# A fused attention and token-mixing kernel: q in 6 KB rows, x transposes inside attention, later loads on ScalarE's queue

## The chip, the cores and the metric

One core of one Trainium2 chip. The metric is the device time of one execution in microseconds (us), as the median of several. A run counts as slow when it is over 1.5% above the fastest of the same kernel. The rounds ran on different chips, so each run is compared with before in its own rounds. A difference of under 2% is called "within 2%".

## The reference, cut to what matters

Attention with 16 query heads and 4 key heads over 8 batches of 384 tokens (head size 64), whose result x (384 x 1024 per batch) goes through a token mixer: two thin projections, a 384 x 384 token matrix made of them, a rectifier, and a 1024 x 1024 output projection.

```python
scores = scale * np.matmul(q, k.transpose(0, 1, 3, 2))     # per head
attn = softmax(scores); attn_out = np.matmul(attn, v)
x = attn_out.transpose(0, 2, 1, 3).reshape(B, S, H * D)    # 8 x 384 x 1024
wq = x @ w_q; wk = x @ w_k                                 # 1024 -> 64
W_tok = scale * np.einsum('bsd,btd->bst', wq, wk)
mixed = np.einsum('bst,btd->bsd', W_tok, x)
return np.maximum(mixed, 0.0) @ w_out
```

## The kernel before

The program is a list scheduler in Python: it keeps estimated clocks of the engines and decides in which fixed order TensorE gets its work. Per batch, 36 scores matmuls fill 18 slots of PSUM (the memory, in banks, that TensorE writes its results to) that ScalarE turns into exponentials, 12 groups of 12 matmuls by v follow, and VectorE divides each group by its row sums and writes it to `xnat` in SBUF (the on-chip memory of the operands) as bf16. The tokens are spread so that partition p holds the tokens 3p, 3p+1 and 3p+2. The parts that the argument needs:

```python
def load(b):                       # all on SyncE's queue; q rows of 3 x 64 floats, 768 bytes
    def ld(dst, src, a, z, c0=0, c1=C):
        nc.sync.dma_start(out=dst[:, a:z, c0:c1],
                          in_=src[b, a:z].rearrange("h (p c) d -> p h c d", p=P)[:, :, c0:c1])
...
def attend(b, g, u):               # 12 times a batch
    xnats[b] = x_p.tile([P, C, Hq, D], BF16, name="xnat", bufs=3)
    ...
    avv = ps[:, :G * DE].rearrange("p (i e) -> p i e", i=G)
    nc.vector.reciprocal(out=rcp, in_=avv[:, :, D])
    nc.vector.tensor_tensor(out=xnats[b][:, c, h0:h0 + G, :], in0=avv[:, :, :D],
                            in1=rcp.to_broadcast([P, G, D]), op=ALU.mult)   # 256 neighbours
...
def po():                          # output projection and store
    dst = out[b].rearrange("(p c) n -> c p n", c=C)[c]      # 128 rows of 4 KB
    ...
    nc.sync.dma_start(out=dst, in_=osb)
...
wld[:, dc:dc + 2, :] <- moe_w_out[dc * P:(dc + 2) * P, :].rearrange("(c p) n -> p c n", p=P)   # shortened
```

The softmax here doesn't subtract the row's maximum and nothing guards it: scores larger than these inputs give would overflow.

## Time and profile before

| | before |
|---|---|
| median of 3 runs | 224.09 us (223.12 to 225.83) |
| span of the profiled execution | 224.3 us |
| TensorE / VectorE / ScalarE busy | 95% / 65% / 63% |

(The profiled execution took 226.12 us in all and counts as a slow one, so its waits may be a little longer than those of a median run; there is no other profile of before.) The prediction below shows the page's head and the hole at 42.6 to 45.4 us. First, from the page's costliest groups (line, engine, operation, tiles, count, then busy us, mean ns of one, and idle time before it), the two steps of VectorE that finish a group of heads:

```profile
L289 DVE TENSOR_TENSOR xnat<-bank,rcp 128x256 bf16<-128x256 f32 x96 | 40.8, 425 | 3.3
L287 DVE RECIPROCAL rcp<-bank 128x4 f32<-128x4 f32 x96 | 16.9, 176 | 17.6 <-PE bank L282 16.7
```

Second, the busy time of each engine in two whole batches of the steady part (from the first scores of one batch to those of the next):

```profile
core 0: us, PE busy (x) PEld busy (x) DVE busy (x) ACT busy (x) POOL busy (x), PEclk, DMA share, GB/s
91.30:113.00 21.70, 21.38 (x248) 11.32 (x252) 15.49 (x41) 17.39 (x19) 5.32 (x10) 1.00 1.04 258
113.00:134.70 21.70, 21.38 (x245) 11.26 (x248) 14.15 (x39) 17.44 (x19) 5.32 (x10) 1.00 1.08 233
```

A steady batch takes 21.7 us and TensorE is busy in 21.4 of them; over four such batches (68.7 to 156.3 us, 21.9 us each) VectorE works 15.5 us a batch, 71%. That is more than its 65% of the span, since the whole includes stretches where it has little to do.

### The profile page before, as it was taken

How to read it: one execution, taken by the hardware profiler on the slowest of the kernel's cores; microseconds unless marked ns; L12 is line 12 of the kernel's file. 1: busy time of each engine (PE TensorE's matmuls, PEld its weight loads, DVE VectorE, ACT ScalarE, POOL GpSimd, SP SyncE). 2: the span in 40 equal slices, each digit the busy share in tenths (PEclk: the TensorE clock that was granted, in tenths of full speed). 3: DMA queues.
4: the chain of work that ended last, by engine and by line, in shares of the span. 5: the costliest groups of instructions: out<-in, count | busy, mean ns of one | idle time of the engine just before them, and what ended most of it. 6: DMA issues, size and time to landing. Idle time of an engine off the chain costs nothing.

```text
span 224.3 us, 5470 instructions
## 1 busy us (share of the span) xinstructions
PE 214.2 (95%) x2217; PEld 113.6 (51%) x2244; DVE 145.2 (65%) x365; ACT 140.6 (63%) x146; POOL 52.1 (23%) x97
## 2 busy tenths in 40 slices
PE   8999999589999999999999999999999999999993
PEld 5666665245545545454555546554555553434441
DVE  2355786834697758865887648874679569576332
ACT  3599998747788778887887887887888600000000
POOL 1385678406300540045016100620000000000000
PEclk9999999959999999999999999999999999999999
DMA  6996999999399979999999998989224422242424
GB/s 174 324 327 170 410 386 325 136 237 323 65 183 215 335 166 187 222 338 216 223 229 342 154 213 260 281 205 154 99 91 53 143 93 93 93 190 93 180 101 187
DMA packets 71688, 46.09 MB, mean 205 GB/s; under 512 B 42736, under 2 KB 67568, under 8 KB 71664
## 3 DMA queue, kind: packets, MB, share of 16 engines
q1 hardware_dynamic: 71520, 45.62, 77.6%
q8 instruction: 17, 0.28, 0.5%
q10 hardware_dynamic: 144, 0.13, 0.2%
q14 instruction: 7, 0.06, 0.1%
HBM read 23.59 MB, written 12.58 MB: 161 GB/s over the span
## 4 chain that ended last, share of the span: by engine, by line
PE 74%; DMA 14%; DVE 3%; SPq 3%; POOL 3%; issue 1%; DVEq 0%
PE bank L408 37%; PE bank L282 13%; PE sc L259 12%; DMA qraw<-in_q_dram 12%; PE bank L331 4%; SPq L129 3%; PE bank L384 3%; PE bank L362 2%; DMA QT<-qb 2%; PE bank L322 1%; POOL qb L158 1%; DVE osb L421 1%; PE bank L349 1%; DVE msb L389 1%; POOL wqk_sb L596 1%
## 5 line engine op out<-in xcount | busy, mean ns | idle before, releaser
L263 ACT ACTIVATE pt<-sc 128x1024 bf16<-128x1024 f32 x144 | 138.9, 1023 | 34.6 <-PE sc L259 34.4
L408 PE MATMUL bank<-wout_sb,msb 128*128 128x512 bf16 x357 | 91.7, 382 | 1.3 <-issue 0.5
L408 PEld LDWEIGHTS <-msb 128*128 128x128 bf16 x384 | 33.8, 98 | 42.4 <-issue 13.7
L259 PE MATMUL sc<-QT,KT 64*128 64x512 bf16 x288 | 47.5, 387 | 3.1 <-DMA QT<-qb 2.9
L282 PEld LDWEIGHTS <-pt 128*128 128x128 bf16 x1152 | 41.9, 98 | 15.8 <-issue 9.9
L282 PE MATMUL bank<-vext,pt 128*128 128x65 bf16 x1152 | 46.9, 195 | 0.4 <-DVE osb L421 0.2
L421 DVE COPY osb<-bank 128x512 f32<-128x512 f32 (+1 forms) x49 | 33.1, 677 | 21.7 <-PE bank L408 20.5
L289 DVE TENSOR_TENSOR xnat<-bank,rcp 128x256 bf16<-128x256 f32 x96 | 40.8, 425 | 3.3
L389 DVE TENSOR_SCALAR msb<-bank 128x384 bf16<-128x384 f32 x64 | 32.5, 551 | 9.5 <-PE bank L384 9.0
L287 DVE RECIPROCAL rcp<-bank 128x4 f32<-128x4 f32 x96 | 16.9, 176 | 17.6 <-PE bank L282 16.7
L158 POOL CAST qb<-qraw 128x768 bf16<-128x768 f32 x30 | 24.0, 827 | 17.4 <-DMA qraw<-in_q_dram 15.1
L153 POOL CAST kb<-kraw 128x192 bf16<-128x192 f32 x30 | 9.2, 347 | 67.3 <-DMA kraw<-in_k_dram 67.3
L259 PEld LDWEIGHTS <-KT 64*128 64x128 bf16 x288 | 12.4, 94 | 24.1 <-issue 17.2
L117 PE MATMUL bank<-idle 128*128 128x256 bf16 x80 | 14.8, 324 | 1.0 <-DVE idle L562 1.0
L331 PE MATMUL bank<-xT,wqk_sb 128*128 128x384 bf16 x64 | 11.7, 327 | 0.0
L117 PEld LDWEIGHTS <-idle 128*128 128x128 bf16 x80 | 7.9, 114 | 6.6 <-issue 4.0
L384 PE MATMUL bank<-wT,Csb 64*128 64x384 bf16 x32 | 10.6, 332 | 0.4 <-DVE rcp L287 0.3
L384 PE MATMUL bank<-wq,Csb 64*128 64x384 bf16 x32 | 10.6, 332 | 0.0
L599 POOL CAST wout_sb<-wld 128x1024 bf16<-128x1024 f32 x8 | 8.1, 1040 | 4.1 <-DMA wld<-in_moe_w_out_dram 4.1
L366 DVE CAST Csb<-bank 128x512 bf16<-128x512 f32 x8 | 5.5, 688 | 5.2 <-PE bank L362 5.2
L337 DVE CAST wT<-bank 128x384 bf16<-128x384 f32 x8 | 4.5, 558 | 6.7 <-PE bank L331 6.7
L323 DVE COPY xT<-bank 128x1024 bf16<-128x1024 bf16 x10 | 6.9, 688 | 2.5 <-PE bank L322 2.5
(33 smaller groups left out, 70.1 us busy)
## 6 DMA issues: line engine op xcount, KB each, us to landing
out_dram<-osb SPq DMA_DIRECT2D x23, 512.0 KB, 3.1
qraw<-in_q_dram SPq DMA_DIRECT2D x15, 768.0 KB, 7.4
wld<-in_moe_w_out_dram SPq DMA_DIRECT2D x4, 1024.0 KB, 9.5
kraw<-in_k_dram SPq DMA_DIRECT2D x7, 384.0 KB, 4.3
vraw<-in_v_dram SPq DMA_DIRECT2D x7, 384.0 KB, 8.9
qraw<-in_q_dram SPq DMA_DIRECT2D x1, 512.0 KB, 5.3
kraw<-in_k_dram SPq DMA_DIRECT2D x2, 192.0 KB, 3.7
vraw<-in_v_dram SPq DMA_DIRECT2D x2, 192.0 KB, 6.3
```

The costliest lines, as they stand in the source:

```text
L117: nc.tensor.matmul(out=bank_ps[i][:, :256], lhsT=idle[:, :P], rhs=idle, start=True, stop=True)
L158: eng.tensor_copy(out=nats[b][1][:, :, kp, :, u, :].rearrange("p c i d -> p i c d"), in_=raws[b][2][:, h0:h0 + G])
L259: nc.tensor.matmul(out=ps[:, u, :], lhsT=KT[lo:hi, kp * C + kc, :], rhs=QT[lo:hi, t0:t0 + G, :].rearrange("k i p -> k (i p)"), start=True, ...
L263: nc.scalar.activation(out=pt.rearrange("k u i p -> k u (i p)"), in_=ps, func=AF.Exp, scale=attn_scale)
L282: nc.tensor.matmul(out=ps[:, i * DE:i * DE + D + 1], lhsT=tiles[kc][:, u, i, :], rhs=vext[:, 2 * kp + u, kc, :D + 1], start=(kc == 0), sto ...
L287: nc.vector.reciprocal(out=rcp, in_=avv[:, :, D])
L289: nc.vector.tensor_tensor(out=xnats[b][:, c, h0:h0 + G, :], in0=avv[:, :, :D], in1=rcp.to_broadcast([P, G, D]), op=ALU.mult)
L331: nc.tensor.matmul(out=ps, lhsT=wqk_sb[:, dc, :], rhs=xT[:, dc].rearrange("d c p -> d (c p)"), start=(dc == 0), stop=(dc == DC - 1))
L384: nc.tensor.matmul(out=bank_ps[i][:, :S], lhsT=Csb[lo:hi, j * P:(j + 1) * P], rhs=w[lo:hi, :], start=True, stop=True)
L389: nc.vector.tensor_scalar_max(out=msb[:, dc, :], in0=bank_ps[i][:, :S], scalar1=0.0)
L408: nc.tensor.matmul(out=ps, lhsT=msbs[b][:, dc, c * P:(c + 1) * P], rhs=wout_sb[:, dc, half * NH:(half + 1) * NH], start=(nd == 0), stop=(n ...
L421: nc.vector.tensor_copy(out=osb[:, n0:n1], in_=ps[:, n0 - half * NH:n1 - half * NH])
```

## The change

The intent is to remove the hole at batch 2. Its q, k and v are queued at the start, right behind the weights. q is read in contiguous rows: partition = (one of 8 heads, stretch s of 24 tokens), once for each half of the heads, so that a partition reads 24 tokens x 64 floats, 6 KB, in one row. The token order on the partitions changes with that, and so do the rows of a store: partition 16m + s holds token 24s + 8c + m. The weights are read in longer rows too, "(p c)" in place of "(c p)", so the 1024 columns of x must be written in another order, which the multiply does on the way. The x transposes of a batch can start inside its attention, the transposes on TensorE are split into 64-row halves, and the loads of batches 3 to 7 leave from ScalarE's queue. The diff, cut to its core (scheduler estimates and casts left out):

```diff
+    def q_of(b):
+        return nc.sync if b < 3 else nc.scalar
     def load(b):
-        qraw = raw_p.tile([P, Hq, C, D], F32, name="qraw")
+        qraw = raw_p.tile([P, 2, C * M, D], F32, name="qraw")
+        def ld_q(c0, c1):
+            src = q[b].rearrange("(u a) (s t) d -> (a s) u t d", u=2, t=C * M)
+            q_of(b).dma_start(out=qraw[:, :, c0 * M:c1 * M], in_=src[:, :, c0 * M:c1 * M])
 ...
+    def half_trs(srcs):            # transposes as two 64-row tiles in two banks
+        for j, src in enumerate(srcs):
+            for half in range(2):
+                nc.tensor.transpose(out=outs[half][:, j, :], in_=src[lo:hi], identity=ident[lo:hi, lo:hi])
 ...
     def attend(b, g, u):
-            xnats[b] = x_p.tile([P, C, Hq, D], BF16, name="xnat", bufs=3)
+            xnats[b] = x_p.tile([P, C, DC, P], BF16, name="xnat", bufs=3)
+            chain_open(b)
-        nc.vector.tensor_tensor(out=xnats[b][:, c, h0:h0 + G, :], in0=avv[:, :, :D],
-                                in1=rcp.to_broadcast([P, G, D]), op=ALU.mult)
+        r = P // Hq
+        nc.vector.tensor_tensor(
+            out=xnats[b][:, c].rearrange("p e (h r) -> p h r e", r=r)[:, h0:h0 + G],
+            in0=avv[:, :, :D].rearrange("p i (r e) -> p i r e", r=r),
+            in1=rcp.unsqueeze(2).unsqueeze(3).to_broadcast([P, G, r, DC]), op=ALU.mult)
 ...
-        dst = out[b].rearrange("(p c) n -> c p n", c=C)[c]
+        dst = out[b].rearrange("(s c m) n -> c m s n", c=C, m=M)[c]
 ...
-    nc.sync.dma_start(out=wqkld[:, :, 0, :], in_=moe_w_q.rearrange("(c p) h -> p c h", p=P))
+    nc.sync.dma_start(out=wqkld[:, :, 0, :], in_=moe_w_q.rearrange("(p c) h -> p c h", p=P))
 ...  (w_k and w_out alike)
+    load(2)
```

## The prediction

The sum: 4.0 + 2.8 + 3.2 - 1.5 - 0.3 = 8.2 us off 224.1; its last term: 0.3 us for the last store. The rates of 280 and 380 GB/s in (a) are estimates, between and near the slices of 170 and of 386 to 410 GB/s named there. A switch of tiling, which (d) and the fourth rival count, costs about 95 ns in before: from an output matmul to a scores matmul it takes 312 ns start to start, to the next output matmul 216 (medians of its packed trace, 60 to 150 us).

> **What bounds the kernel now.** I read four views of the profile of before in this order: the page's busy shares and strip of slices, the waits, the windows around the one hole in the strip, and the timeline there.
>
> ```profile
> span 224.3 us, 5470 instructions
> PE 214.2 (95%) x2217; PEld 113.6 (51%) x2244; DVE 145.2 (65%) x365; ACT 140.6 (63%) x146; POOL 52.1 (23%) x97
> PE   8999999589999999999999999999999999999993
> ACT  3599998747788778887887887887888600000000
> PEclk9999999959999999999999999999999999999999
> ```
>
> TensorE is the bound on the whole, but not everywhere. ScalarE's row shows 9 only in slices 3 to 6: there batches 0 and 1 run at the pace of the exponentials and TensorE fills up with idle matmuls (80 in the program's order). At slice 8 TensorE falls to 5 and its clock to 5. After that TensorE is full to the end. The list of waits names what stands at that hole, and what holds ScalarE:
>
> ```profile
> ACT pt L263 <- PE sc L259: 34.4, 58, 2.6
> PEld L259 <- DMA KT<-kb: 3.3, 1, 3.3
> PE sc L259 <- DMA QT<-qb: 2.9, 1, 2.9
> ```
>
> ```profile
> 42.00:43.00 1.00, 0.58 (x8) 0.12 (x4) 0.93 (x5) 1.00 (x2) 0.40 (x1) 1.00 0.07 7
> 43.00:44.00 1.00, 0.00 (x0) 0.00 (x0) 1.00 (x3) 0.55 (x1) 0.00 (x0) 1.00 1.63 204
> 44.00:45.00 1.00, 0.00 (x0) 0.00 (x0) 0.08 (x1) 0.00 (x0) 0.00 (x0) 0.58 0.91 199
> 45.00:46.00 1.00, 0.55 (x3) 0.14 (x3) 0.00 (x0) 0.00 (x0) 0.00 (x0) 0.50 1.26 279
> ...
> 50.00:51.00 1.00, 1.00 (x3) 0.44 (x3) 0.00 (x1) 0.99 (x1) 0.22 (x1) 0.51 1.07 356
> 51.00:52.00 1.00, 0.92 (x7) 0.14 (x6) 0.00 (x0) 0.07 (x1) 1.00 (x4) 1.00 1.06 330
> ```
>
> (Columns: busy PE, PEld, DVE, ACT, POOL, then granted clock, DMA share, GB/s.) TensorE stands still from 42.6 to 45.4 us, and then works at half clock until 51.0. The timeline tells why: batch 2's q was cast late and its transposing DMA left late.
>
> ```profile
> 22.77 8.86 SPq L129 DMA_DIRECT2D qraw<-in_q_dram  x2
> 39.90 1.60 POOL L158 CAST qb<-qraw 128x768 bf16<-128x768 f32 x2 [0.60 <-DMA qraw<-in_q_dram]
> 41.53 2.62 SPq L195 DMA_TRANSPOSE QT<-qb  x2
> 45.45 0.61 PE L259 MATMUL sc<-QT,KT 64*128 64x512 bf16 x2 [2.87 <-DMA QT<-qb]
> ```
>
> So the time is 45.45 us to the first scores of batch 2, plus 178.85 us of TensorE work after it. In that second part the waits of TensorE for anything but its own issue sum to about 1 us between 52 and 222 us, so it is the sum of the work.
>
> [...]the clock fell about 1.8 us after the last matmul and took 5.5 us of work to return. [...]The new stores have a slowest dimension of 8 on the output side (8x16x1024 in the order, 128x1024 before)[...]. [...]two 64-row score matmuls of 512 columns take 0.27 us together (0.54 for x4), a full-row matmul of 512 columns 0.218 us (x40 in 8.74). [...]The new moving operand of the scores is read in runs of 16 bf16 (32 bytes)[...].
>
> **The change part by part.**
>
> (a) The loads. Batch 2's load is moved from inside batch 1 to the head of the queue, right behind the weights; q goes in 6 KB rows (2 KB for batch 0) instead of 768 bytes, w_q and w_k in 2 KB rows instead of 256. The slices of before moved 170 GB/s where the w_q and w_k rows were in flight and 386 to 410 where w_out's 4 KB rows were. Up to the end of load 2 there are 3 x 2.25 MB + 0.5 + 4 = 11.25 MB. Estimate: k and v (2.25 MB) at 280, the rest (9 MB) at 380 GB/s is 8 + 24 = 32 us, from 1.2 us: q of batch 2 lands at 33 to 34, its casts on GpSimd (6 x about 0.55) are through by 37, and the first QT part, needed alone, is cast at 35 and lands 3.7 us after issue, at 39. It is needed at about 41.4 (next). So the wait and the half clock go.
>
> (b) The exponential stage. 14 exponentials took 13.34 us, 0.953 each; 36 take 34.3. They ran from 7.55 to 43.55 = 36.0, so there were about 1.95 us of gaps: 1.06 at 10.4 us (the next q stretch was not there) and 0.89 at 34.1 (the eight wqk matmuls ahead of a score). The new order goes by q stretch first, both halves of the heads at once, so after three exponentials the next three need only the second k pair, landing at about 6.6 us: the first gap goes, the second half stays. The start itself: the first q piece doubles (512 KB instead of 256) but in 2 KB rows; casts of 512 columns for 256 and two copies for one cost up to 0.6 us, the k pair and 64-row transposes give some back. I take 0 to 0.3 later. The score slot of batch 2 was free at 42.6 in before; in after at 42.6 - 1.06 - 0.3 + 0.2 = 41.4. Against 45.45: 4.0 us.
>
> (c) Half clock: 45.45 to 51.0 is 5.55 us at 0.5, so 2.8 us come back.
>
> (d) Work after the first scores of batch 2, counted in the two orders: 384 output matmuls left in before, 380 in after (4 x 0.218 = 0.9). Seven x transposes of 8 full matmuls, 0.544 us start to start, against nine of 16 half ones; half the columns and two row tiles at once, an estimate of 0.26 each: 3.8 - 2.4 = 1.4. Seven wk transposes, 0.18 to about 0.10: 0.6. Five idle matmuls become two: 0.3. Tiling switches 140 to 137: nothing. Sum 3.2.
>
> (e) Costs. 15 load issues go to ScalarE, 3 in a batch, for batches 3 to 7. An unblocked issue took 0.37 (the one on ScalarE's queue) to 0.58 us, so 1.4 us in a batch. ScalarE waited 25.5 us for TensorE between 52 and 180 us, so the room is there, but the three come in one piece between two exponentials; the order gives two to four output matmuls more there. I charge 0.3 us a batch, 1.5. The wider split of transposes costs VectorE 2 x 0.43 for 0.69, 0.17 each: hidden at 65% busy. The scattered writes of xnat I take as free: 256 elements in 425 ns[...].[...]
>
> Sum: 4.0 + 2.8 + 3.2 - 1.5 - 0.3 = 8.2; 224.1 - 8.2 = 215.9. I predict 215.7.
>
> **The rivals.**
>
> First: batch 2 is still late. If the loads run at 300 GB/s, 11.25 MB take 37.5 us, q lands at 40 and the first scores come at 45 again with the half clock. For it: the mean over the first 39 us was 300. Against it: those 39 us contain the 256-byte and 768-byte rows, and the k and q of batch 2 are now queued without waiting for batch 1. It would leave only (d) and give 222.
>
> Second: ScalarE becomes the new wait. If a load issue on its queue takes 1 to 2 us, as those on SyncE did when the queue was backed up (0.96 to 8.86), 3 to 5 us in each of five batches stand between two exponentials and TensorE, whose order is fixed, waits: 5 to 12 us, and the gain is gone, 219 to 226. Against it: far fewer rows are in flight then, and it has its own queue.
>
> Third: the strided operands are not free. If the xnat write cost doubled, VectorE would gain 96 x 0.27 = 26 us and run at 80%, still below TensorE, with waits for banks of perhaps 3 us: 219. If the scores slowed by a tenth, 216 of them x 0.0135 = 3 us.
>
> Fourth, upward: more of the chain of batches 0 and 1 lies inside the ScalarE-bound stage than I counted, or steady batches lose less to switches: 212.
>
> **Range and chances.** Around 215.7; first rival one in ten, second in a mild form one in six, third one in ten. The range of 8 in 10 is 212.0 to 219.5. Two per cent faster is below 219.6: 0.88. Within two per cent: 0.10. Slower: 0.02.
>
> **What would show it.** The strip should have no fall of PE or of PEclk at slice 8, no wait of the scores for QT, and the first scores of batch 2 at 41 to 42 us. The first seven slices should move more than 300 GB/s on the mean. The x-transpose line should show 64-column matmuls at about half the time per batch. ScalarE's queue should show 15 loads of about 0.5 us, and ScalarE waits of TensorE's scores no longer than 2 us each in batches 3 to 7. Wrong if the hole stays, if the scores or the xnat multiply have a longer mean (387 and 425 ns now), or if new idle time of TensorE stands right behind the load issues.

## More of the kernel before

Third, the stores land 3.1 us after issue (median of the page's DMA issues):

```profile
out_dram<-osb SPq DMA_DIRECT2D x23, 512.0 KB, 3.1
```

## The result, and the profile after

| | median | range | runs |
|---|---|---|---|
| before, same rounds | 223.61 us | 222.86 to 225.83 | 4 |
| after | 273.43 us | 272.16 to 274.4 | 4 |

The ratio is 1.2205 (95% interval 1.2101 to 1.2308): 22% slower, where 3.7% faster was predicted. Ratios here are the mean time of one kernel's fast runs over that of the other's fast runs of the same rounds, so they are not quite the ratio of the medians quoted. The profiled execution of after is a fast one, and the results agree with the reference. Its page begins:

```profile
span 272.5 us, 5840 instructions
PE 222.1 (81%) x2377; PEld 111.2 (41%) x2405; DVE 218.5 (80%) x384; ACT 142.3 (52%) x146; POOL 53.3 (20%) x110
PE   5969877867987986989778987887997978799970
DVE  2398986998999889889888979999996999776330
DVE 60%; PE 32%; issue 3%; DMA 2%; ACT 0%; SPq 0%; DVEq 0%
```

TensorE has no single hole any more, but is short of full nearly everywhere, and VectorE has become dense. The last line is the chain of work that ended last, by engine: VectorE holds 60% of the span (before: TensorE 74%, VectorE 3%). The groups that answer to those of before:

```profile
L316 DVE TENSOR_TENSOR xnat<-bank,rcp 128x256 bf16<-128x256 f32 x96 | 124.5, 1297 | 4.4
L313 DVE RECIPROCAL rcp<-bank 128x4 f32<-128x4 f32 x96 | 26.3, 274 | 4.1 <-PE bank L308 3.8
L283 PE MATMUL sc<-QT,KT 64*128 64x512 bf16 x288 | 48.3, 393 | 0.4
```

The multiply that writes x takes 1297 ns where it took 425, for the same 256 elements: 3.05 times. The scores, whose operand is strided now too, went from 387 to 393: nothing. A stretch of the timeline shows how the long multiply reaches TensorE (start, duration, engine, line, then in brackets the idle time before and what ended it):

```profile
102.18 0.17 DVE L313 RECIPROCAL rcp<-bank 128x4 f32<-128x4 f32 x1
102.38 1.29 DVE L316 TENSOR_TENSOR xnat<-bank,rcp 128x256 bf16<-128x256 f32 x1
103.30 0.38 DVE L313 RECIPROCAL rcp<-bank 128x4 f32<-128x4 f32 x1
103.73 0.32 PE L410 MATMUL bank<-wT,Csb 64*128 64x384 bf16 x1 [0.59 <-DVE rcp L313]
103.74 1.30 DVE L316 TENSOR_TENSOR xnat<-bank,rcp 128x256 bf16<-128x256 f32 x1
104.66 1.22 DVE L415 TENSOR_SCALAR msb<-bank 128x384 bf16<-128x384 f32 x2
105.47 0.99 PE L308 MATMUL bank<-vext,pt 128*128 128x65 bf16 x24 [0.43 <-DVE msb L415]
```

VectorE passes from one record to the next without a gap. From one multiply to the next it takes 1.36 us (102.38 to 103.74), against 0.54 in before (99.94 to 100.48). TensorE wants a bank that VectorE has still to empty, and waits 0.43 and 0.59 us in this stretch alone. The record of the reciprocal right behind a multiply is longer too (0.38 against 0.17), but it starts while that of the multiply still runs, so its 0.2 us are no cost on top. The windows of two steady batches, columns as before, give the balance:

```profile
83.50:112.80 29.30, 24.57 (x267) 12.19 (x267) 26.17 (x46) 17.44 (x18) 5.52 (x12) 1.00 0.83 176
112.80:141.40 28.60, 23.98 (x263) 11.89 (x265) 24.93 (x43) 17.44 (x18) 5.58 (x12) 1.00 0.76 183
```

Over four batches (83.5 to 200.5 us) one takes 29.25 us. VectorE is busy for 26.2 of them, 10.7 more than before, and 12 multiplies at 0.872 us more are 10.5. So VectorE alone needs more than the 21.9 us that a whole batch took before; in the other 3.1 us of the 29.25 it waits.

The time lost by stages: the first scores of batch 2 start at 56.2 us in place of 45.5 (+10.7), those of batch 7 at 200.5 in place of 156.3 (another +33.5), the last matmul ends at 263.8 in place of 220.7 (1.1 less than that), and from there to the end it takes 8.7 us in place of 3.6 (+5.2). The sum, 48.3 us, is the difference of the spans (272.5 - 224.3) to rounding.

And yet the part of the change that I had worked out most closely did what it should. The loads of batch 2 in after:

```profile
35.60 3.40 POOL L186 CAST qb<-qraw 128x512 bf16<-128x512 f32 x6 [1.95 <-DMA qraw<-in_q_dram]
36.80 3.98 SPq L223 DMA_TRANSPOSE QT<-qb  x3
```

q is cast from 35.6 us on, where before cast its second half at 39.9, and its transposes leave at 36.8, not 41.5. By then nobody is waiting for them.

### The profile page after: what moved, and what is told of

Same layout as the page of the kernel before. It is cut to its first block, busy times and chain, and to the rows that moved or that the text cites. A ratio compares the mean times of both kernels' runs of the same rounds, so it can differ in the third digit from the quotient of the medians.

```text
span 272.5 us, 5840 instructions
## 1 busy us (share of the span) xinstructions
PE 222.1 (81%) x2377; PEld 111.2 (41%) x2405; DVE 218.5 (80%) x384; ACT 142.3 (52%) x146; POOL 53.3 (20%) x110
## 4 chain that ended last, share of the span: by engine, by line
DVE 60%; PE 32%; issue 3%; DMA 2%; ACT 0%; SPq 0%; DVEq 0%
DVE xnat L316 40%; PE bank L434 17%; DVE msb L415 6%; PE sc L283 4%; DVE osb L447 4%; DVE rcp L313 3%; PE bank L308 3%; PE bank L131 2%; PE bank L388 2%; DVE xT L246 2%; PE bank L240 2%; PE bank L410 2%; DMA qraw<-in_q_dram 2%; DVE Csb L392 1%; DVE wq L364 1%
## 5 line engine op out<-in xcount | busy, mean ns | idle before, releaser
L288 ACT ACTIVATE pt<-sc 128x1024 bf16<-128x1024 f32 x144 | 140.4, 1021 | 81.7 <-PE sc L283 80.6
L316 DVE TENSOR_TENSOR xnat<-bank,rcp 128x256 bf16<-128x256 f32 x96 | 124.5, 1297 | 4.4
L283 PE MATMUL sc<-QT,KT 64*128 64x512 bf16 x288 | 48.3, 393 | 0.4
L447 DVE COPY osb<-bank 128x512 f32<-128x512 f32 (+1 forms) x49 | 35.3, 723 | 11.1 <-PE bank L434 11.0
L415 DVE TENSOR_SCALAR msb<-bank 128x384 bf16<-128x384 f32 x64 | 35.6, 598 | 3.4 <-PE bank L410 3.0
L186 POOL CAST qb<-qraw 128x512 bf16<-128x512 f32 x45 | 25.8, 619 | 23.3 <-DMA qraw<-in_q_dram 13.3
L313 DVE RECIPROCAL rcp<-bank 128x4 f32<-128x4 f32 x96 | 26.3, 274 | 4.1 <-PE bank L308 3.8
L283 PEld LDWEIGHTS <-KT 64*128 64x128 bf16 x288 | 10.6, 94 | 23.2 <-issue 21.2
L410 PE MATMUL bank<-wq,Csb 64*128 64x384 bf16 x32 | 10.5, 329 | 4.7 <-DVE rcp L313 3.7
L246 DVE COPY xT<-bank 128x512 bf16<-128x512 bf16 x24 | 9.4, 434 | 4.7 <-PE bank L240 4.7
L240 PE MATMUL bank<-ident,xnat 64*128 64x64 bf16 x192 | 5.2, 191 | 6.7 <-DVE xnat L316 5.7
L388 PE MATMUL bank<-xnat,wkN 128*64 128x512 bf16 x48 | 7.4, 417 | 2.8 <-DVE wkN L377 1.7
```

The source lines that it names most:

```text
L186: copy(out=nats[b][1][:, c * M:(c + 1) * M, u, :], in_=raws[b][2][:, u, c * M:(c + 1) * M])
L246: nc.vector.tensor_copy(out=dst[:, :, half * H:(half + 1) * H], in_=outs[half][:, n0:n1, :])
L283: nc.tensor.matmul(out=ps[:, u, :], lhsT=KT[lo:hi, kp * C + kc, :], rhs=QT[lo:hi, c * M:(c + 1) * M, kp * H:(kp + 1) * H].rearrange("k m ( ...
L288: nc.scalar.activation(out=pt.rearrange("k u i p -> k u (i p)"), in_=ps, func=AF.Exp, scale=attn_scale)
L316: nc.vector.tensor_tensor(out=xnats[b][:, c].rearrange("p e (h r) -> p h r e", r=r)[:, h0:h0 + G], in0=avv[:, :, :D].rearrange("p i (r e) ...
L410: nc.tensor.matmul(out=bank_ps[i][:, :S], lhsT=Csb[lo:hi, j * P:(j + 1) * P], rhs=w[lo:hi, :], start=True, stop=True)
```

## The experiments

Theories for the loss. S (scatter): the multiply is slow since each bf16 that it writes lands 256 bytes from the last, with no neighbour written in turn (an estimate from its two times: (1297 - 425) / 256 = 3.4 ns more for each element); VectorE so becomes the bound. Its rivals: the form of the operands (four dimensions, a broadcast in two of them) is slow by itself; only a step that is a power of two, as 256 bytes is, is slow; and, apart from the multiply, the loads on ScalarE's queue (Q), the stores on 8 engines, or the new order of TensorE's work cost the time. ("On 8 engines" and "on 16 engines" stand for what the packed traces show: eight updates of the semaphore when the data of a store of after lands, sixteen for a store of before. That each update is one DMA engine is the author's reading.)

### e1: the same write, in runs of 8 neighbours

```diff
-            out=xnats[b][:, c].rearrange("p e (h r) -> p h r e", r=r)[:, h0:h0 + G],
-            in0=avv[:, :, :D].rearrange("p i (r e) -> p i r e", r=r),
-            in1=rcp.unsqueeze(2).unsqueeze(3).to_broadcast([P, G, r, DC]), op=ALU.mult)
+            out=xnats[b][:, c].rearrange("p e (h r) -> p h e r", r=r)[:, h0:h0 + G],
+            in0=avv[:, :, :D].rearrange("p i (r e) -> p i e r", r=r),
+            in1=rcp.unsqueeze(2).unsqueeze(3).to_broadcast([P, G, DC, r]), op=ALU.mult)
```

Every element goes to the same address as in after; only the order of the loops differs, so that eight neighbours are written in turn, and the step of 8 elements moves to the read from PSUM.

> The changed kernel with the loops of the xnat multiply swapped, so that it writes runs of 8 neighbours (16 bytes) and reads PSUM in steps of 8; same layout, right result, same order on TensorE. Theory S[...]: an eighth as many jumps, the multiply takes 0.45 to 0.6 us for 1.30, the following instruction loses its extra 0.2 us, and the time is 214 to 222 us. Rival F (the four-dimensional access, the broadcast or the wide spread of the destination is what is slow, however it is walked): 1.3 us and 273 us as in the changed kernel.

Measured: 237.8 us median (231.7 to 240.17); before in the same rounds 223.89. Three of the four runs are over 1.5% above the fastest and count as slow, so no ratio is given. The multiply is back at 425 ns:

```profile
L316 DVE TENSOR_TENSOR xnat<-bank,rcp 128x256 bf16<-128x256 f32 x96 | 40.8, 425 | 3.3
```

So the scatter is shown to be the largest part: about 32 us lie even between e1's slowest run and after's fastest. But e1 is still slower than before, and its strip (of a slow run; the fast run profiled for e2 shows the same) has a new hole:

```profile
PE   5999999999999998999999989904999999999940
PEclk9799999999999999999999999985899999999996
```

Around it (windows, then the timeline of SyncE's queue and of the scores that ended the hole):

```profile
152.00:156.00 4.00, 1.61 (x7) 0.52 (x7) 1.76 (x4) 1.65 (x2) 0.00 (x0) 1.00 1.09 196
156.00:160.00 4.00, 0.00 (x0) 0.00 (x0) 0.00 (x0) 0.00 (x0) 0.00 (x0) 0.71 1.70 211
160.00:164.00 4.00, 0.75 (x4) 0.28 (x6) 0.00 (x0) 0.04 (x1) 0.27 (x1) 0.50 0.57 85
```

```profile
137.36 4.82 SPq L223 DMA_TRANSPOSE QT<-qb  x1
152.66 8.92 SPq L342 DMA_TRANSPOSE xT<-xnat  x1
163.25 1.03 PE L283 MATMUL sc<-QT,KT 64*128 64x512 bf16 x4 [9.64 <-DMA QT<-qb]
163.73 3.42 POOL L186 CAST qb<-qraw 128x512 bf16<-128x512 f32 x6 [15.81 <-issue]
```

TensorE, VectorE and ScalarE all stand still from about 153 to 163 us, and half clock follows (0.50 in the last of these windows). The DMA engines are busy, though: an x transpose takes SyncE's queue 8.92 us to issue, and the packets of batch 7's q are spread over 17.4 us. The scores that waited are the last third of batch 6 (240 of the 288 scores matmuls, 36 a batch, lie before them). They need the last part of batch 6's QT, whose transposing DMA was issued at 137.36. By the semaphore updates in the packed trace it landed at 163.20, 25.8 us later (median in before 3.7), and the scores started at 163.25. A store issued at 142.27 landed at 164.2. Batch 7's q, cast from 163.7 on, was late too, but it was not what these scores waited for. So transfers, not engines, were late. There is also a long end: 9.4 us from the last matmul to the end of the span.

### e2: the natural order of x, with the weights in rows "(c p)"

```diff
+            out=xnats[b][:, c].rearrange("p a b -> p (a b)").rearrange("p (h r e) -> p h r e", r=r, e=DC)[:, h0:h0 + G],
-    ... moe_w_q.rearrange("(p c) h -> p c h", p=P) ...   (w_k and w_out alike)
+    ... moe_w_q.rearrange("(c p) h -> p c h", p=P) ...
```

The views keep four dimensions and the double broadcast of after, but their 256 elements are neighbours.

> The changed kernel with x in its natural order of features, written in one contiguous piece by the same four-dimensional views, and the weight rows taken as before the change. All else of the change stays. Theory S: multiply at 0.43 us, time 213 to 219 us, as the rest of the prediction said (215.7). Rival F: multiply stays at 1.3 us. Rival R (the rest of the change also costs: loads on ScalarE's queue, transposes of half height, stores on 8 engines): multiply at 0.43 us, but the time stays above 226 us.

Measured: 239.58 us (239.1 to 241.43), ratio 1.0717 (1.0651 to 1.0783), multiply 425 ns. The form of the operands is free here (425 ns, as in before), so that rival falls. e2 has e1's hole in the same slices, in a fast run, so the hole has nothing to do with how x or the weights lie. The time is what rival R said.

### e3: the scatter alone, put into before

```diff
 (before)
-            xnats[b] = x_p.tile([P, C, Hq, D], BF16, name="xnat", bufs=3)
+            xnats[b] = x_p.tile([P, C, DC, P], BF16, name="xnat", bufs=3)
-        nc.vector.tensor_tensor(out=xnats[b][:, c, h0:h0 + G, :], ...
+        nc.vector.tensor_tensor(out=xnats[b][:, c].rearrange("p e (h r) -> p h r e", r=r)[:, h0:h0 + G], ...
 (and the three weights in rows "(p c)", which this order of x needs)
```

> The kernel before with one part of the change alone: the scattered write of xnat and the weight rows that go with it. Theory S: multiply at 1.30 us, VectorE at 80% or more, 96 times about 1.07 us more work on VectorE, time 260 to 280 us. Rival R: the multiply alone hurts less than half, time under 245 us.

Measured: 266.93 us (266.17 to 269.25), ratio 1.1941 (1.1863 to 1.2019).

```profile
L290 DVE TENSOR_TENSOR xnat<-bank,rcp 128x256 bf16<-128x256 f32 x96 | 124.5, 1297 | 4.4
DVE 56%; PE 41%; issue 2%; DVEq 0%
```

The same 1297 ns and the same chain through VectorE, without any of the new loads, stores or orders: 43 us by itself.

### e4: the write by itself, at other steps

Appended to e2, behind all its work: groups of six multiplies or copies of 256 fp32 from PSUM to scratch memory, each with another step.

```diff
+    for _ in range(REP):
+        tt(view(8), src(8))       # 16 bytes from one write to the next
+    for _ in range(REP):
+        tt(view(128), src(128))   # 256 bytes
+    for _ in range(REP):
+        tt(*runs(2))              # two neighbours, then 256 bytes on
+    ...
```

> The kernel of the natural order with a row of small multiplies appended after its end, six of each form, on VectorE and some on ScalarE: 256 elements from PSUM with the innermost step of the destination 2, 4, 8, 16, 32, 64, 128, 256 and 264 bytes, runs of 2, 4 and 8 at 256 bytes, a strided read with a contiguous write, fp32 at 512 bytes, a copy at 256 bytes, ScalarE at 256 bytes. Theory S: flat at about 0.42 us up to some step, then up to 1.3 us; 264 bytes as slow as 256; runs of 8 near 0.5. Rival B (only a step that is a power of two, 256 bytes, is slow[...]): 264 bytes near 0.42 us, 256 at 1.3. Rival F: the form alone (three loops, broadcast) is slow, at every step.

One run (322.98 us, the appended work included), read from its trace. Mean ns of one instruction:

| bf16 written | ns | | bf16 written | ns |
|---|---|---|---|---|
| 256 neighbours | 424 | | step 128 bytes | 1295 |
| step 4 bytes | 442 | | step 256 bytes | 1295 |
| step 8 bytes | 716 | | step 264 bytes | 1253 |
| step 16 bytes | 1278 | | runs of 2, 256 bytes apart | 425 |
| step 32 bytes | 1226 | | runs of 4 or 8 | 424 |
| step 64 bytes | 1266 | | strided read, writes to neighbours | 424 |

Three of these as the trace has them (number of records in the window, then shortest, median and longest duration in ns) are the steps of 8 and of 16 bytes and the runs of two:

```profile
L688 DVE TENSOR_TENSOR wld<-bank,one x5: 716/716/716, 233.3 to 236.3; 128x256 bf16<-128x256 f32 x5
L688 DVE TENSOR_TENSOR wld<-bank,one x5: 1277/1278/1279, 237.8 to 243.0; 128x256 bf16<-128x256 f32 x5
L688 DVE TENSOR_TENSOR wld<-bank,one x5: 424/424/425, 285.6 to 287.4; 128x256 bf16<-128x256 f32 x5
```

The power-of-two theory falls: 264 bytes, which is no multiple of a power of two above 8, is nearly as slow as 256 (1253 against 1295 ns). From 16 bytes on, the price hardly moves: an estimate from the table is (1278 - 424) / 256 = 3.3 ns more for each element. S holds for lone elements, but in a narrower form than I had put it: two neighbours, 256 bytes from the next two, cost nothing more (425 against 424 ns). What costs is a bf16 written without a neighbour, when the next is 8 bytes on (716 ns) or 16 and more (1226 to 1295). The operation and the engine do not matter much (a copy of VectorE, then two of ScalarE, with the step of 256 bytes and with neighbours):

```profile
L725 DVE CAST wld<-bank 128x256 bf16<-128x256 f32 x6 | 7.8, 1293 | 0.2
L727 ACT CAST wld<-bank 128x256 bf16<-128x256 f32 x6 | 7.8, 1295 | 113.0 <-DVE wld L725 112.9
L729 ACT CAST wld<-bank 128x256 bf16<-128x256 f32 x6 | 2.2, 372 | 0.2
```

A lone fp32 at a step of 512 bytes took 586 ns, less than half of a lone bf16's time, and lone bf16 at a step of 4 bytes only 442; the mechanism inside was not shown and stays open.

### e5: all loads of e1 on SyncE's queue

The rest, 237.8 against 223.9, is next. Q says that the loads on ScalarE's queue make the hole.

```diff
 (e1)
-        return nc.sync if b < 3 else nc.scalar
+        return nc.sync
```

> The run-of-8 write order, with every load on SyncE's queue instead of ScalarE's for batches 3 to 7. Theory Q (loads on a second queue interleave with the transposing DMAs of SyncE's queue and both crawl: 146 to 162 us moved about 110 GB/s, and batch 7's q came so late that the scores waited 9 to 10 us and the clock halved): the wait of the scores for QT goes, no half clock near 170 us, the time falls by about 13 us to 222 to 228 us. Rival E (the stores on 8 engines are what delays the loads): the wait stays, over 232 us. The tail between the last matmul and the end stays at about 9 us in both.

Measured: 235.55 us (233.45 to 237.1), ratio 1.0572 (1.049 to 1.0654) against 222.35. The one long hole goes, and three waits of the scores for QT, up to 3.9 us each, come in its place (in its profile, of a slow run). Q falls as the cause of the loss. Two readings in the text above are wrong: the stretch from 146 to 162 us of e1 moved 146 GB/s on the mean, not 110, and the scores waited for a part of batch 6's QT, not for batch 7's q.

### e6: e1 with the stores on 16 engines

```diff
 (e1)
-        dst = out[b].rearrange("(s c m) n -> c m s n", c=C, m=M)[c]
+        dst = out[b].rearrange("(c p) n -> c p n", c=C)[c]
```

The rows land in the wrong order: the store is 128 rows of 4 KB in a piece, as large as before, but its slowest dimension is 128, not 8. (The comparison with the reference let even this pass, so it says nothing of row order in what follows.)

> The run-of-8 write order, loads still on ScalarE's queue, but each store goes to 128 neighbouring rows[...], which puts rows in wrong places: a wrong result on purpose. Theory T (stores on 8 engines drain at about 150 GB/s, which the last 35 us of output matmuls just fill, so a backlog is left at the end): the time from last matmul to end falls from about 9 to about 3.6 us, time lower by 5 to 7 us if the wait for QT stays (Theory Q), about 18 lower if it goes too (Rival E).

Measured: 218.37 us (217.52 to 218.81), ratio 0.9837 (0.9799 to 0.9874). The hole is gone, the clock is full throughout and the tail is 3.8 us, not 9.4. So the stores, not the loads, cost e1 its time: 13 us between the slowest run of e6 and the fastest of e1, 19 between the medians.

The packed traces tell the two kinds of store apart. Every store of after, e1, e2, e5 and e12, with 8 as its slowest dimension, has nine updates of its semaphore, one about 1 us or more after issue and eight when data lands; every store of before, e6, e10 and e13, with 128 or 16, has sixteen. (The 150 GB/s of Theory T is what e1 moved near its end: 151 from 220 to 228 us.) A whole store lands 7.0 us after issue in after (median; the shortest 5.9), against 3.1 in before (2.6) and 3.4 in e6 (2.6).

### e7: before, with the loads of batches 3 to 7 on ScalarE's queue

```diff
 (before)
-            nc.sync.dma_start(out=dst[:, a:z, c0:c1],
+            (nc.sync if b < 3 else nc.scalar).dma_start(out=dst[:, a:z, c0:c1],
```

> The kernel before with one part of the change alone: the loads of batches 3 to 7 issued on ScalarE's queue. Theory Q: transposes and loads slow each other, and the scores of some batch wait for QT: 227 to 240 us. Rival E or A (ScalarE's issues cost nothing, the queue is harmless with stores on 16 engines): within 1% of 224.

Measured: 244.89 us (243.93 to 246.14), ratio 1.1027 (1.0972 to 1.1082). With the 768-byte rows of before the issues are not short:

```profile
94.97 1.70 ACTq L129 DMA_DIRECT2D qraw<-in_q_dram  x2
96.76 3.84 ACTq L129 DMA_DIRECT2D vraw<-in_v_dram  x1
100.70 2.85 ACT L263 ACTIVATE pt<-sc 128x1024 bf16<-128x1024 f32 x3 [5.31 <-DMA kraw<-in_k_dram]
```

ScalarE's own queue is blocked while it issues, and its next exponential starts 5.31 us late. The time is over both ranges, and Theory Q's way is not what is seen: the scores wait 17.6 us in all for exponentials and only 2.5 for QT. In after, with q in 6 KB rows, 12 of the 15 issues take 0.37 to 0.65 us, the longest 2.36. So the second rival of the prediction is real. That the longer rows of q keep it away is likely but not shown: k and v keep 768-byte rows in after, the order differs too, and no run changes the rows alone.

### e8: the last stores cut into eight

```diff
 (e1, loads on SyncE)
-            nc.sync.dma_start(out=dst, in_=osb)
+            if b >= B - 3:
+                for m in range(M):   # 16 rows each
+                    ....dma_start(out=dst[m], in_=osb[m * 16:(m + 1) * 16, :])
```

This keeps the right rows, and each piece has a slowest dimension of 16.

> A right result with all three repairs: run-of-8 write order, loads on SyncE, and the stores of the last three batches cut into 8 of 16 rows each[...]. Theories S, Q and T together: tail near 4 us, no wait for QT, 214 to 221 us, so faster than before. If the many small stores fill SyncE's queue and delay its transposes: 222 to 230.

Measured: 249.59 us (248.88 to 252.42), ratio 1.1259 (1.1179 to 1.1339): a miss. The tail grew to 17.9 us.

```profile
224.72 15.15 SPq L456 DMA_DIRECT2D out_dram<-osb  x19
```

19 issues took 15.15 us, 0.8 us each, so eight pieces take 6.4 us of issue, while TensorE makes the output of one whole store in about 3.5 us (16 matmuls of 0.216). This repair pays for its smaller pieces with too many issues. It also leaves the stores of the first five batches with 8 as their slowest dimension, and the strip of e8 still falls to 5 and to 3 at two places in the middle.

### e10 and e11: stores on 16 engines, meant for the right rows

The order of rows can be turned inside the chip, where it cost nothing here (550 ns a rectifier, 551 in before): the rectifier of VectorE reads its PSUM bank with a stride and writes `msb` in the order (c, s, m), so that partition 8s + m of the product holds token 24s + 8c + m, and a store is 16 x 8 x 1024.

```diff
 (e1)
-            nc.vector.tensor_scalar_max(out=msb[:, dc, :], in0=bank_ps[i][:, :S], scalar1=0.0)
+            nc.vector.tensor_scalar_max(out=msb[:, dc, :].rearrange("p (c s m) -> p c s m", c=C, m=M),
+                                        in0=bank_ps[i][:, :S].rearrange("p (c m s) -> p c s m", c=C, m=M), scalar1=0.0)
-        dst = out[b].rearrange("(s c m) n -> c m s n", c=C, m=M)[c]
+        dst = out[b].rearrange("(s c m) n -> c s m n", c=C, m=M)[c]
```

> A right result with both repairs: run-of-8 write of xnat, and msb written with its columns in the order (chunk, stretch, token), read strided from PSUM, so that the store has 16 as its slowest dimension (16x8x1024) and the same rows of the output as the changed kernel. Loads stay on ScalarE's queue. Theory E (8 engines for the stores, not the rows they go to, cost about 19 us): 215 to 220 us as the wrong-result run of 16 engines (218.4), tail under 4.5 us, no half clock, msb at 551 ns as before. Rival D (the rows, 8 stretches apart in HBM, are slow): 230 us or more.

e11 is e10 with the edit of e5 (all loads on SyncE's queue).

> The repaired kernel with all loads on SyncE's queue: the worth of the move to ScalarE's queue by itself. If ScalarE's queue is worth something (loads need not stand behind stores that wait for their data in SyncE's order): 2 to 8 us slower than the repaired kernel, with waits of the scores for QT or KT. If it is worth nothing: within 1.5 us.

Measured, six runs each, before in the same rounds 224.15: e10 219.28 us (217.96 to 220.92), ratio 0.982 (0.9755 to 0.9885); e11 219.63 us (218.11 to 220.32), ratio 0.9836 (0.9782 to 0.989). e10 is the fastest version meant to be right, 1.8% under before by its ratio (the interval holds 2%, so it stays unclear whether it is faster by more), and the queue of the later loads is worth nothing that six runs show. (SyncE's queue does stand waiting for the data of stores: in before 53.4 us, in 16 waits.) Rival D falls: the rows are those of after. The new order of TensorE's work and the halved transposes, suspects at the start, are in e10 too, and it is below before with them. A store of e10 lands after 4.5 us (median). That e10's rows are right rests on the algebra of the indices, since the comparison passed e6 too. Its page:

```profile
span 217.4 us, 5868 instructions
PE 209.7 (96%) x2405; PEld 109.7 (50%) x2405; DVE 146.1 (67%) x384; ACT 140.6 (65%) x146; POOL 53.2 (24%) x110
PE   6999999999999999999999999999999999999991
PEclk9999999999999999999999999999999999999999
L415 DVE TENSOR_SCALAR msb<-bank 128x384 bf16<-128x384 f32 x64 | 32.5, 550 | 6.2 <-PE bank L410 5.8
```

TensorE is full from the second slice to the last but one at full clock, and the strided read of the rectifier is free (551 ns in before). The tails of after and of e10, as windows from about the last matmul to the end:

```profile
264.00:272.50 8.50, 0.00 (x0) 0.00 (x0) 0.56 (x2) 0.00 (x0) 0.00 (x0) 0.63 0.35 107
213.00:217.40 4.40, 0.00 (x0) 0.00 (x0) 0.73 (x2) 0.00 (x0) 0.00 (x0) 1.00 0.51 156
```

### e12 and e13: the other two corners

e12 is before with the stores of after (wrong rows); e13 is after, scatter and all, with the 16-engine stores of e10.

```diff
 (e12: before)
-        dst = out[b].rearrange("(p c) n -> c p n", c=C)[c]
+        dst = out[b].rearrange("(s c m) n -> c m s n", c=C, m=8)[c]
 (e13: after, with the two edits of e10)
```

> The kernel before with one part of the change alone: stores with 8 as the slowest dimension, to the rows that the changed kernel writes (a wrong order of rows on purpose). Theory E: tail from the last matmul to the end 9 us for 3.6, and later loads or transposes; 230 to 245 us. Rival: only the tail, 228 to 231.

> The changed kernel with the stores on 16 engines and the scattered write left as it is. VectorE bounds it (1.3 us a multiply and 0.2 more in the next), so the loads have time: only the tail goes, 5 to 6 us, 265 to 269 us. If the two costs simply add: 253 us.

Measured: e12 249.32 us (245.82 to 250.24), ratio 1.1076 (1.0965 to 1.1187), its profiled run a slow one and the time above Theory E's range; e13 269.72 us (268.25 to 270.39), ratio 1.2072 (1.1994 to 1.215), 0.7 above its range and far from simple addition. The 8-engine stores cost before 25 us at one stroke, and the strip and the waits of e12 show how:

```profile
PE   8999998999999939999899649993999999999950
PE sc L259 <- DMA QT<-qb: 16.7, 5, 5.7
```

The scores of five batches wait 16.7 us in all for transposed q. So the two causes, in medians:

| | stores on 8 engines | stores on 16 engines |
|---|---|---|
| x written one by one, 256 bytes apart | 273.4 (after) | 269.7 (e13) |
| x written in runs of 8 | 237.8 (e1) | 219.3 (e10) |

They do not add up. Under the scatter the stores cost 3.7 us, without it 18.5 (12.4 if e1's only fast run, 231.7, is taken): at VectorE's slower pace most of the slow transfers is hidden, which is the likely reading. What stays open is how stores on 8 engines, transposes and loads come to crawl together in the middle of the kernel: the runs show that the stores cause it, not the path by which they do.

## Why the prediction was wrong, point by point

(a), the loads: right, in after itself, about a microsecond late. q of batch 2 was cast from 35.6 us on (predicted 35), its transposes left at 36.8, the first part of QT landed at 40.0 (predicted 39), and no hole stood at slice 8.

(b), first scores of batch 2 at 41.4: 56.2 in after, since VectorE already held batches 0 and 1 back. In e10, where the two causes are away, it is 42.9: the first scores of all started 0.6 us later than in before, and I had allowed 0.3. So 2.5 us gained of the predicted 4.0. (Two slips of the prediction: in (b), 36.0 less 34.3 is 1.7 us of gaps, not 1.95; and the clock fell 1.6 us after the end of the last matmul, 42.58 to 44.15, not 1.8.)

(c) and (d), the half clock and less work on TensorE: from the first scores of batch 2 to the last matmul I expected 6.0 us less, minus 1.5 for issues, 4.5. In e10 it is 170.0 against 175.3, 5.3 less, at full clock. The single terms were not measured apart; one of them is off, since 16 half transposes mostly take 0.33 us from their start to that of the next work, not my 0.26. That the sum came so near is in part luck: the profile of before is a slow run, and the spans differ by 6.9 us where the medians differ by 4.9. So with both wrong terms repaired, e10 (219.28) still stands 3.6 us above 215.7 (the sum itself said 215.9), and the fourth rival, 212, is not seen.

(e), the costs, is where it failed, in two terms. "The scattered writes of xnat I take as free" is the main one. The reason given was a rate, 256 elements in 425 ns; measured on neighbours, it says nothing of writing lone bf16: 1297 ns, 43 us in e3, 50.4 between e13 and e10. That the scores, whose operand is read in runs of 16 elements, would not slow down held (387 to 393 ns); of lone writes, which the multiply now makes, I had no measurement. The second term is the charge for the last store on 8 engines, 0.3 us. The number of engines came out as I had supposed, going by the updates; the effect was sized for the last store alone, when all 24 stores of the kernel have it. It is 5.2 us in the tail of after, and 12 to 18.5 us in all between e1 and e10.

The rivals. The first (batch 2 late) did not occur. The second (ScalarE's issues) costs no more than was charged in the repaired kernel (e10 against e11), and costs before 22.5 us (e7). The third named the right instruction and the right sign of danger, "If the xnat write cost doubled", but had three mistakes of size: the multiply took three times as long, not twice; doubling it would add 96 x 0.425 = 41 us, not the 96 x 0.27 = 26 of the text; and it held VectorE's share of the whole span, 80%, to be "still below TensorE". VectorE in after is in fact 80% busy over the span, but that is chance: 73 us more work on a span 48 us longer. Within a steady batch it had 15.5 of 21.9 us before, so doubling the multiply (12 x 0.425 more) would have made it 20.6, 94%, and hardly any slack would be left in TensorE's fixed order (an argument; no run doubles it); the measured 26.2 is past the old length of a batch. A share of the span averaged that away.

## What to carry to other kernels

When a layout change makes an engine write 2-byte elements one at a time to scattered places, look for the loop order in which at least two neighbours are written in turn, and put the stride on the PSUM read: the same data then cost 425 ns in place of 1297. Look at the slowest dimension of every store in the loop, not of the last one alone (8 in place of 16 took e1 12 to 18.5 us longer than e10), and compare an engine's new load with its slack in one steady stage. After a change with several parts, a table of two by two tells whether one cause hides another.
